# Chunked attention and top-128 mixture-of-depths on one core: the step order written out as a list, V turned back by transposes with separate gate products, 66-column values

## The chip, the cores and the metric

One Trainium2 chip, one of its cores. The metric is device time in microseconds of one execution. The engines are TensorE (PE, with its weight loads shown as PEld), VectorE (DVE), ScalarE (ACT), GpSimd (POOL) and SyncE (SP). Each takes its instructions in the order in which the program issues them, and waits for semaphores of the others. DMAs are issued from POOL (loads, which also turn f32 into f16, gathers and scatters) and from SP (the small loads and the stores).

## The reference

Two stages. First attention in chunks of 32 queries over 768 positions, for 4 batches and 8 heads of 64; each chunk sees 16 positions to its left, itself, 8 to its right, and 8 memory positions.

```python
for c in range(nc):                                   # 24 chunks
    l_start, r_end = max(0, c*32 - 16), min(S, c*32 + 32 + 8)
    k_full = concat([mem_k, k[:, :, l_start:r_end]]); v_full = ...
    a = exp(s - max(s)),  s = q_c @ k_full.T / sqrt(D)
    out[:, :, chunk] = (a / (sum(a) + 1e-9)) @ v_full
```

Its output, with the heads side by side, is x of shape 4 x 768 x 512. Then a routed feed-forward: the 128 positions of each batch with the highest gate score get one.

```python
scores = einsum('bsd,d->bs', x, w_gate)
top = 128 positions with the largest scores[b]
h = maximum(x[b, top] @ w1, 0)                        # 512 -> 1024
out[b, top] = x[b, top] + sigmoid(scores[b, top]) * (h @ w2)
```

## The kernel before

The attention is worked in 16 pairs of heads (NPR = 16, four pairs to a batch). The steps of pair n, by the names of the functions:

- `load` (L92, L96): three DMAs of POOL bring q, k and v into the tiles ldq, ldk and ldv, ten buffers each.
- `t_q`, `c_q`: sixteen PE transposes of q into a bank of PSUM (t, two of them), then two copies, one per head, into the block-diagonal tile qbd (64x384 words of 32 bits), one on ACT and one on DVE (the copying helper is L83 for ACT, L85 for DVE and POOL).
- `t_w`, `c_w`, `m_w` for K and for V: sixteen transposes, one copy into the window tile kw or vw (128x672 words), and a small copy that puts the memory rows in (128x96 words), on POOL.
- `scores` (L258, 26 products), `maxima` (L267, DVE), `sub_max` (L274, two products that add the negative maximum), `expo` (L279, ACT).
- `v_back` (L301): V's windows lie transposed and are turned back by products with a constant tile mvw of 66 columns: the identity and two columns of gate weights. Two halves of twelve products each; `c_vs` copies each half into vs as f16, 128x792 numbers, the first half on ACT, the second on DVE.
- `p_trans`, `c_p`: six transposes of the probabilities, two copies into ptd (64x384 words).
- `values` (L319): 24 products of 67 columns (64 values, two gate columns, a column of ones for the sum); `normal` (L330, L331, L333, DVE) divides into x and into the gate scores gb.

The score tiles, the turned-back V, the probabilities and the values all take one of three double banks w in turn.

Per batch follows the routing: `m_score` sums the gate scores, `m_rows` (L363) transposes them to rows, `m_brow` copies, `m_cmp` (L389, six DVE compares of 768), `m_count` (L397, 36 products of one column), `m_mask`, `m_pref`, `m_select`, `m_aux`, `m_index`, then `m_fetch` gathers the rows (an indirect DMA of POOL), `m_xt` transposes them, `m_ffn1` (L473), `m_relu`, `m_ffn2` (L488), `m_y`, `m_scatter` (L501). For the last batch the rows are picked by products (`m_cast`, `m_pick`, L456) and the scatter adds.

The order is that of one loop, `for i in range(-2, NPR)`: iteration i issues the scores of pair i+1, the values of pair i, the transposes of pair i+2, and a share of the routing of the batch before and of the feed-forward of the one before that (`pieces`). Before the loop the loads of pairs 0 to 8 are issued; after it come batch 2's feed-forward and then all of batch 3's routing. Banks go round by counters (`nw`, `nt`).

Of the kernel before, what the change touches and what calls it, by code (L numbers as in the profile page):

```python
# [25 lines left out]

@with_exitstack
def kernel(  # L30
# [13 lines left out]
    nc = tc.nc  # L44
# [16 lines left out]
    VC = 67  # L61
# [63 lines left out]
    filler(2, 6)  # L125

    ident = cst.tile([128, 128], FP, tag="ident")
    make_identity(nc, ident)
    ident16 = cst.tile([128, 128], F16, tag="ident16")
    DVE.tensor_copy(out=ident16, in_=ident)  # L130
    load("q", 1)
    load("k", 1)
    load("v", 1)
    for t in T:
        DVE.memset(t[:, 0:400], 0.0)
    qbds = [cst.tile([128, NCH, 64], F16, tag=f"qbd{i}", name=f"qbd{i}") for i in range(3)]
    ptds = [cst.tile([128, 6, 4, 2, 32], F16, tag=f"ptd{i}", name=f"ptd{i}") for i in range(3)]
    vss = [cst.tile([128, 12, 2, 68], F16, tag=f"vs{i}", name=f"vs{i}") for i in range(3)]
    for t in qbds:
        DVE.memset(t[0:64, :, 32:64], 0.0)  # L140
        DVE.memset(t[64:128, :, 0:32], 0.0)
    perm16 = cst.tile([128, 128], F16, tag="perm16")
    DVE.tensor_copy(out=perm16.rearrange("p (a t j) -> p a t j", t=4, j=8),
                    in_=ident16.rearrange("p (a j t) -> p a t j", t=4, j=8))
    for t in ptds:
        DVE.memset(t[0:64, :, :, 1, :], 0.0)
        DVE.memset(t[64:128, :, :, 0, :], 0.0)

    slot_i = cst.tile([128, 3], I32, tag="slot_i")
    slot_m = cst.tile([128, 2], FP, tag="slot_m")  # L150
    POOL.iota(slot_i[:, 0:1], pattern=[[0, 1]], base=0, channel_multiplier=1)
    DVE.tensor_scalar(out=slot_i[:, 1:2], in0=slot_i[:, 0:1], scalar1=15, scalar2=None, op0=ALU.bitwise_and)
    DVE.tensor_scalar(out=slot_i[:, 2:3], in0=slot_i[:, 0:1], scalar1=14, scalar2=None, op0=ALU.bitwise_and)
    DVE.tensor_scalar(out=slot_m[:, 0:1], in0=slot_i[:, 1:2], scalar1=3.5, scalar2=None, op0=ALU.is_gt)
    DVE.tensor_scalar(out=slot_m[:, 1:2], in0=slot_i[:, 2:3], scalar1=12.0, scalar2=None, op0=ALU.not_equal)
    for t in vss:
        DVE.memset(t[:, :, :, 66:67], 1.0)
        DVE.tensor_copy(out=t[0:64, 0, :, 66:67], in_=slot_m[0:64, 0:1].unsqueeze(1).to_broadcast([64, 2, 1]))
        DVE.tensor_copy(out=t[64:128, 11, :, 66:67], in_=slot_m[64:128, 1:2].unsqueeze(1).to_broadcast([64, 2, 1]))

    warm = cst.tile([128, 1], FP, tag="warm")
    DVE.memset(warm, 0.0)
    ACT.activation(out=warm, in_=warm, func=AF.Exp, scale=1.0)

    memT = []
    for i in range(2):
        p_m = one(3 + i)[:, 0:128]
        PE.transpose(out=p_m, in_=mem32[i].rearrange("p h d -> p (h d)"), identity=ident)
        mt = cst.tile([128, NPR, 4, 2], F16, tag=f"memT{i}", name=f"memT{i}")
        ACT.copy(out=mt, in_=p_m.rearrange("p (n g j) -> p n j g", n=NPR, j=4))  # L170
        memT.append(mt)

    mvw = cst.tile([128, NP, 66], F16, tag="mvw")
    wgc = cst.tile([128, NP], FP, tag="wgc")

    def gate_weights():
        p_w = one(2)[:, 0:NP]
        PE.transpose(out=p_w, in_=wg4, identity=ident[0:4, 0:4])
        DVE.tensor_copy(out=wgc, in_=p_w)
        for h in range(2):  # L180
            o = 64 * h
            POOL.tensor_copy(out=mvw[o:o + 64, :, 0:64], in_=ident16[o:o + 64, o:o + 64].unsqueeze(1).to_broadcast([64, NP, 64]))
        DVE.tensor_copy(out=mvw[:, :, 64], in_=wgc)
        DVE.tensor_tensor(out=mvw[:, :, 65], in0=wgc, in1=mvw[:, :, 64], op=ALU.subtract)
# [7 lines left out]
    def route_consts():  # L192
# [101 lines left out]
    def v_back(n, half, wi):  # L294
        vw = vws[n]
        w = two(wi)
        for i in range(6):
            P = 6 * half + i
            for h in range(2):
                o = 64 * h  # L300
                PE.matmul(out=w[:, h, 66 * i:66 * i + 66], lhsT=vw[o:o + 64, 2 * P:2 * P + 2].rearrange("p c j s -> p (c j s)"),  # L301
                          rhs=mvw[o:o + 64, n % NP, :], start=True, stop=True)
        pvs[n, half] = w

    def c_vs(n, half, e):
        copy(e, vss[n % 3][:, 6 * half:6 * half + 6, :, 0:66].rearrange("p i h d -> p h i d"),
             pvs[n, half][:, :, 0:396].rearrange("p h (i d) -> p h i d", d=66))
# [364 lines left out]
```

## Time and profile before

| what | value |
|---|---|
| times of three runs | 196.89 us median (195.09 to 199.99) |
| the profiled execution's own time | 197.33 us |
| its span, first to last instruction | 195.6 us |
| mean granted TensorE clock | 0.776 |
| instructions | 5672 |

The span is what all rows of the profile refer to; the rest of the own time lies around it. In the rows of groups, "busy, mean ns | idle before" tells how long an engine worked on a kind of instruction and how long it had stood before it, with the one that ended the wait. Rows of the timeline begin with the start and the length in microseconds.

### The profile page before, as it was taken

The page shows a single profiled execution, that of the slowest core. Times are in us where ns is not written, and L with a number is a line of the kernel's source. Part 1 is how long each engine was busy: PE and PEld are TensorE (multiplying, and loading weights), DVE is VectorE, ACT ScalarE, POOL GpSimd, SP SyncE. Part 2 cuts the span into 40 slices and gives each one's busy share as a digit, 9 for nine tenths or more (in the row PEclk, how much of TensorE's full clock was granted, in tenths as well). Part 3 has the DMA queues.
Part 4 walks back from the last instruction along what each step waited for, and adds up shares of the span by engine and source line. Part 5 has one row for each costly group of instructions (what it writes and reads, how often), then busy time and mean ns, then how long its engine had stood idle before and what let it go on. Part 6 is the DMA issues. An engine that isn't in the chain of part 4 may idle for free. (4 is left out here: it accounts for less than half of the span.)

```text
span 195.6 us, 5672 instructions
## 1 busy us (share of the span) xinstructions
PE 121.0 (62%) x2481; PEld 93.0 (48%) x2481; DVE 121.0 (62%) x259; ACT 60.8 (31%) x101; POOL 60.6 (31%) x113
## 2 busy tenths in 40 slices
PE   5401068567687488889687579895776537516750
PEld 1301046445465467667474458684645436204620
DVE  1872038877855998778429969664599830596010
ACT  2011025365245251541621632534333402100210
POOL 7996697643560000065000501200003020340020
PEclk9999999999658855555869975558899555965797
DMA  3999999999999200029920100730001055000003
GB/s 60 182 197 197 198 198 199 204 201 171 133 298 230 38 3 3 3 42 284 246 38 3 55 3 3 250 129 0 3 0 57 3 179 196 35 18 3 2 0 54
DMA packets 22288, 20.15 MB, mean 103 GB/s; under 512 B 1780, under 2 KB 18168, under 8 KB 22264
## 3 DMA queue, kind: packets, MB, share of 16 engines
q0 software_dynamic: 18416, 13.37, 44.8%
q1 hardware_dynamic: 3848, 6.43, 9.1%
q8 instruction: 19, 0.31, 0.6%
q14 instruction: 5, 0.04, 0.1%
HBM read 23.99 MB, written 7.34 MB: 160 GB/s over the span
## 5 line engine op out<-in xcount | busy, mean ns | idle before, releaser
L501 POOL DMA_INDIRECT out_dram<-y,idx x4 | 5.0, 1261 | 68.6 <-ACT kw L83 40.9
L83 ACT COPY qbd<-t 64x384 uint32<-64x384 uint32 x16 | 7.6, 472 | 47.9 <-PE t L211 47.9
L267 DVE TENSOR_REDUCE nm<-w 128x12 f16<-128x768 f32 x16 | 15.3, 957 | 10.5 <-PE w L258 10.1
L319 PE MATMUL w<-vs,ptd 128*64 128x67 f16 x384 | 12.1, 226 | 15.8 <-DVE ptd L85 15.8
L85 DVE CAST vs<-w 128x792 f16<-128x792 f32 x16 | 15.7, 980 | 8.8 <-PE w L301 8.7
L319 PEld LDWEIGHTS <-ptd 128*64 128x64 f16 x384 | 10.0, 137 | 17.6 <-DVE ptd L85 17.6
L258 PE MATMUL w<-kw,qbd 128*64 128x64 f16 (+2 forms) x416 | 11.7, 214 | 10.2 <-POOL kw L85 10.1
L301 PEld LDWEIGHTS <-vw 64*128 64x128 f16 x384 | 9.4, 108 | 17.6 <-issue 16.8
L301 PE MATMUL w<-mvw,vw 64*128 64x66 f16 x384 | 12.2, 214 | 8.5 <-ACT pp L279 8.5
L473 PE MATMUL w<-xeT,w_sb 128*128 128x128 f16 x128 | 12.4, 275 | 5.5 <-ACT hT L480 2.8
L258 PEld LDWEIGHTS <-qbd 128*64 128x64 f16 x416 | 10.0, 131 | 12.1 <-issue 11.1
L83 ACT CAST vs<-w 128x792 f16<-128x792 f32 x16 | 13.1, 819 | 7.8 <-PE w L301 7.8
L482 DVE TENSOR_SCALAR hT<-w 128x512 f16<-128x512 f32 x4 | 2.8, 692 | 20.6 <-PE w L473 20.6
L437 POOL DMA_INDIRECT xe<-out_dram,idx x3 | 3.1, 1037 | 39.6 <-DVE nm L267 21.0
L333 DVE TENSOR_TENSOR x<-w,rd 128x768 f32<-128x768 f32 x16 | 15.2, 948 | 0.0
L473 PEld LDWEIGHTS <-w_sb 128*128 128x128 f16 x128 | 11.6, 129 | 6.9 <-issue 6.9
L227 PE MATMUL t<-ident,ldv 96*64 96x96 f16 x256 | 10.7, 241 | 5.8 <-DVE qbd L85 5.8
L85 DVE COPY vw<-t 128x672 uint32<-128x672 uint32 x16 | 13.6, 849 | 0.9 <-PE t L227 0.9
L279 ACT ACTIVATE pp<-w 128x768 f16<-128x768 f32 x16 | 13.0, 814 | 3.5 <-PE w L274 3.4
L389 DVE TENSOR_SCALAR gtm<-brow,scr 128x768 f16<-128x768 f32 x24 | 14.0, 633 | 0.1
L85 DVE COPY qbd<-t 64x384 uint32<-64x384 uint32 x16 | 9.0, 561 | 6.1 <-ACT qbd L83 5.8
L211 PE MATMUL t<-ident,ldq 96*64 96x96 f16 x256 | 11.9, 249 | 0.9 <-issue 0.9
(94 smaller groups left out, 245.5 us busy)
## 6 DMA issues: line engine op xcount, KB each, us to landing
out_dram<-x SPq DMA_DIRECT2D x12, 512.0 KB, 5.3
ldq<-in_q_dram POOLq DMA_DIRECT2D x16, 192.0 KB, 6.8
ldk<-in_k_dram POOLq DMA_DIRECT2D x16, 192.0 KB, 7.2
ldv<-in_v_dram POOLq DMA_DIRECT2D x16, 192.0 KB, 7.5
w_sb<-in_moe_w_dram POOLq DMA_DIRECT2D x8, 256.0 KB, 8.2
mem<-in_mem_k_dram SPq DMA_DIRECT2D x2, 32.0 KB, 2.6
mem<-in_mem_v_dram SPq DMA_DIRECT2D x2, 32.0 KB, 4.0
out_dram<-y,idx POOLq DMA_INDIRECT x4, 3.7
```

The source lines that it names most:

```text
L83: ACT.copy(out=out, in_=in_)
L85: ENG[e].tensor_copy(out=out, in_=in_)
L211: PE.transpose(out=tb[64 * h:64 * h + 64, j // 2, j % 2, :], in_=src[:, h, 64 * j:64 * j + 64], identity=ident16[0:96, 0:96])
L227: PE.transpose(out=tb[64 * h:64 * h + 64, j, 4 + 96 * f:100 + 96 * f], in_=src[:, 2 * h + f, 64 * j:64 * j + 64], identity=ident16[0:96, 0 ...
L258: PE.matmul(out=o_, lhsT=qb[:, c, :], rhs=r_, start=(u % 6 == 0 and i == 0), stop=False, skip_group_check=True)
L267: DVE.tensor_reduce(out=nm, in_=sps[n][:, :, 0:384].rearrange("p h (g k) -> p h g k", k=64), axis=AX.X, op=ALU.max, negate=True)
L279: ACT.activation(out=pp.rearrange("p (b u) k -> p b (u k)", b=2), in_=sps.pop(n)[:, :, 0:384], func=AF.Exp, scale=0.125)
L301: PE.matmul(out=w[:, h, 66 * i:66 * i + 66], lhsT=vw[o:o + 64, 2 * P:2 * P + 2].rearrange("p c j s -> p (c j s)"), rhs=mvw[o:o + 64, n % N ...
L319: PE.matmul(out=w[64 * cp:64 * cp + 64, g // 3, u:u + VC], lhsT=pt[:, g, 2 * cp + h].rearrange("p x q -> p (x q)"), rhs=vs[:, 2 * g + cp, ...
L333: DVE.tensor_tensor(out=xs[b][:, :, 128 * pr:128 * pr + 128].rearrange("p (b g) (h d) -> p b g h d", b=2, h=2), in0=p[:, :, :, :, 0:64], i ...
L389: ENG[e].tensor_scalar(out=m.gtm[:, bl, :], in0=m.brow, scalar1=m.scr[:, bl:bl + 1], scalar2=None, op0=ALU.is_lt)
L473: PE.matmul(out=m.p_h[:, half, fi, :], lhsT=w1_sb[:, dch, f0:f0 + 128], rhs=m.xeT[:, dch, :], start=(dch == 0), stop=(dch == 3))
```

## The change

The loop and `pieces` are gone. All work is cut into some 560 steps, and a string `ORDER` names them in the order of issue, with the bank (a digit) or the engine (A for ACT, V for DVE, G for POOL) of each; a function `run` looks each name up. The digits are pairs or batches: `S8:2` is scores of pair 8 in bank 2, `VB` v_back, `VG` the gate products, `CS` the copy into vs, `GS` the sum of gate products, `PT`/`CP` the probabilities, `VA`/`NR` values and normal, `LQ LK LV` loads, `TQ CQ TK CK MK TV CV MV` the transposes, copies and memory rows, `RB BR CM CT MS PP SL PA IX GX XT XE F1 RL F2 YY SX` the routing and feed-forward in the order of the names above, `Z` zero products.

Further, by parts:

- **V back.** `v_back` is 24 f16 transposes into one double bank, 32 words a block; one copy of 128x768 words (`c_vs`) takes the place of the two halves. The gate weights leave that tile: `v_gate` issues twelve products of four columns (two heads, each weight in two f16 parts), `g_sum` adds them on DVE.
- **66 columns.** values has 64 values, one gate column and the ones.
- **Engines.** 17 of the 64x384 copies are on DVE and 47 on ACT (32 and 32 before); 27 of the K and V copies on ACT and 5 on DVE (16 and 16); 19 of the memory-row copies on DVE and 13 on POOL (all 32 on POOL); 15 of the 16 copies into vs on ACT.
- **Zero products.** 18 at the start instead of 6, and six single ones near the end.
- **Small loads.** mem_v is loaded from ACT's queue, mem_k and the gate weights from SP's as before.
- **Feed-forward.** Batch 0's is issued among pairs 12 to 14; batch 1's and 2's after the last values.

```diff
-    for i in range(-2, NPR):
-        a, c, z = pieces(i) if i >= 0 else ([], [], [])
...
+ORDER = """
+Z:2,12 ZT LQ0 LK0 ID I Z:1,6 TQ0:0 ZQ0 CQ0b:A LV0 ZQ1 ZQ2 ZP0 MT0:2 MT1:3 MC1 WR MC0 LK1 LK2 LV1 GT0:4 TK0:1
+CQ0a:V TV0:0 CV0:A CK0:V MV0:V MK0:V GW ZP1 TK1:1 CK1:A S0:3 TK2:0 CK2:A LQ1 LV2 LQ2 VB0:2 MX0 MK2:V ZP2 SI
...
+VB15:3 VG15 PT15:1 PA2:4 CS14:A CS15:A CP15a:A CP15b:A GS14 CP14a:V CP14b:V IX2 GS15 VA14:2 Z:0,1 VA15:4 X60:G
+GX1 XT1:0 XE1:A GX2 Z:1,2 F11:3 NR14 NR15 SC3 RB3:2 BR3:V CM31:V CM33:V CM35:V CM34:V CM32:V CM30:V XT2:1
...
+    def v_back(n, wi):
+        vw = vws[n]
+        w = two(wi)
+        for P in range(12):
             for h in range(2):
                 o = 64 * h
-                PE.matmul(out=w[:, h, 66 * i:66 * i + 66], lhsT=vw[o:o + 64, 2 * P:2 * P + 2].rearrange("p c j s -> p (c j s)"),
-                          rhs=mvw[o:o + 64, n % NP, :], start=True, stop=True)
+                PE.transpose(out=w[:, h, 32 * P:32 * P + 32].bitcast(F16),
+                             in_=vw[o:o + 64, 2 * P:2 * P + 2].rearrange("p c j s -> p (c j s)"),
+                             identity=ident16[o:o + 64, o:o + 64])
+    def v_gate(n):
+        vw = vws.pop(n)
+        for P in range(12):
+            PE.matmul(out=pvs[n][:, 0, 384 + 4 * P:388 + 4 * P],
+                      lhsT=vw[:, 2 * P:2 * P + 2].rearrange("p c j s -> p (c j s)"),
+                      rhs=wgb[:, n % NP, :], start=True, stop=True)
+    def c_vs(n, e):
+        copy(e, vss[n % 3][:, :, :, 0:64].bitcast(U32).rearrange("p i h d -> p h i d"),
+             pvs[n][:, :, 0:384].rearrange("p h (i d) -> p h i d", d=32).bitcast(U32))
+    def g_sum(n):
+        gp = pvs[n][:, 0, 384:432].rearrange("p (i t h) -> p i h t", t=2, h=2)
+            DVE.reduce_sum(out=vss[n % 3][:, :, :, 64:65], in_=gp, axis=AX.X)
```

Where rows stand, engine by engine. First POOL's queue at the start. Before, the last of 27 loads and the first copies of memory rows, which belong to pairs 0 and 1 (kw is K's window tile, memT the transposed memory rows):

```order
L92 DMA ldq_224<-in_q_dram 96x2x512
L96 DMA ldk_226<-in_k_dram 96x4x256
L96 DMA ldv_228<-in_v_dram 96x4x256
L85 COPY kw_264<-memT0_162 128x96
L85 COPY vw_283<-memT1_165 128x96
```

Now, from the sixth load on; the first copy here is that of pair 1, pair 0's having gone to DVE:

```order
L128 DMA ldv_182<-in_v_dram 96x4x256
L124 DMA ldq_294<-in_q_dram 96x2x512
L128 DMA ldv_296<-in_v_dram 96x4x256
L124 DMA ldq_298<-in_q_dram 96x2x512
L653 IOTA slot_i_104 128x1
L117 COPY kw_248<-memT0_107 128x96
L128 DMA ldk_331<-in_k_dram 96x4x256
```

The first copy stands behind nine loads instead of 27, and loads follow it.

Second, DVE in the middle, between two maxima (nm). Before, one pair in early iterations:

```order
L267 TENSOR_REDUCE nm<-w_78 128x12
L330 RECIPROCAL rd<-w_79 128x12
L331 TENSOR_TENSOR gb<-w_79,rd 128x6x4
L333 TENSOR_TENSOR x_460<-w_79,rd 128x6x128
L85 COPY qbd_119<-t_75 64x24x16
L85 CAST vs_127<-w_78 128x2x6x66
L85 COPY vw<-t_75 128x96x7
L85 COPY ptd_124<-w_79 64x24x16
```

Now, from the maxima of pair 7 on:

```order
L302 TENSOR_REDUCE nm<-w_78 128x12
L354 TENSOR_REDUCE vs_103<-w_79 128x24
L377 RECIPROCAL rd<-w_77 128x12
L378 TENSOR_TENSOR gb<-w_77,rd 128x6x2
L380 TENSOR_TENSOR x_1482<-w_77,rd 128x6x128
L377 RECIPROCAL rd<-w_79 128x12
L378 TENSOR_TENSOR gb<-w_79,rd 128x6x2
L380 TENSOR_TENSOR x_1482<-w_79,rd 128x6x128
L117 COPY kw<-memT_107 128x96
L354 TENSOR_REDUCE vs_101<-w_77 128x24
```

The copy into vs and that of vw are gone from here; the sum of gate products (into vs, 128x24) and a copy of memory rows have come, and two pairs' normal stand together.

Third, DVE at the end, where the last batch's scores (scr) are summed. Before:

```order
L357 TENSOR_REDUCE scr<-gb 128x6
L482 TENSOR_SCALAR hT<-w_78 128x512
L494 SCALAR_TENSOR_TENSOR y<-w_79,gate,xe 128x512
L378 TENSOR_SCALAR gt<-gt 128x6
L379 RECIPROCAL gt<-gt 128x6
L381 CAST aux_174<-gt 128x6
L382 TENSOR_TENSOR aux_174<-gt,aux_174 128x6
L389 TENSOR_SCALAR gtm<-brow,scr 128x768 x6
```

Now:

```order
L449 TENSOR_REDUCE scr<-gb 128x6
L117 COPY brow<-w_77 128x768
L481 TENSOR_SCALAR gtm<-brow,scr 128x768 x6
L575 TENSOR_SCALAR hT<-w_79 128x512
L587 SCALAR_TENSOR_TENSOR y<-t_75,gate,xe 128x512
L495 TENSOR_SCALAR mask<-w_77 128x6
```

Batch 2's relu (hT) and its y no longer stand ahead of the compares (gtm), and the four instructions of the gate (gt, aux) have moved behind the selection; the row copy (brow) has come over from ACT.

On PE the same place reads: the row transposes (L455) come after the first half of batch 1's first product (L566), and between them and the counts (L489) stand batch 2's transposes, the other half, both halves of batch 2's first product, and batch 1's second product (L581).

More of the change, by code (lines that the diff above doesn't have):

```diff
@@ L29 @@
+"""
 @with_exitstack
@@ L122 @@
     wg4 = cst.tile([4, 128], FP, tag="wg4")
     SP.dma_start(out=wg4, in_=_dap(moe_w_gate, 0, [[128, 4], [1, 128]]))
-    filler(2, 6)
     ident = cst.tile([128, 128], FP, tag="ident")
-    make_identity(nc, ident)
     ident16 = cst.tile([128, 128], F16, tag="ident16")
[L130 to L135, printed above, removed]
+    perm16 = cst.tile([128, 128], F16, tag="perm16")
     qbds = [cst.tile([128, NCH, 64], F16, tag=f"qbd{i}", name=f"qbd{i}") for i in range(3)]
@@ L154 @@
[L154 to L159, printed above, removed]
@@ L161 @@
-    warm = cst.tile([128, 1], FP, tag="warm")
[L162 to L173, printed above, removed]
@@ L174, with z_t @@
-    wgc = cst.tile([128, NP], FP, tag="wgc")
[L176 to L179, printed above, removed]
+    warm = cst.tile([128, 1], FP, tag="warm")
+    memT = [cst.tile([128, NPR, 4, 2], F16, tag=f"memT{i}", name=f"memT{i}") for i in range(2)]
+    wgb = cst.tile([128, NP, 4], F16, tag="wgb")
+    wgc = cst.tile([128, NP], FP, tag="wgc")
+    p_ms = {}
+    def z_t():
+        for t in T:
+            DVE.memset(t[:, 0:400], 0.0)
@@ new lines, in act_warm, with mem_t, mem_c, g_trans @@
+    def act_warm():
+        ACT.activation(out=warm, in_=zero[:, 0:1], func=AF.Exp, scale=1.0)
+    def mem_t(i, bk):
+        p_ms[i] = one(bk)[:, 0:128]
+        PE.transpose(out=p_ms[i], in_=mem32[i].rearrange("p h d -> p (h d)"), identity=ident)
+    def mem_c(i):
+        ACT.copy(out=memT[i], in_=p_ms[i].rearrange("p (n g j) -> p n j g", n=NPR, j=4))
+    def g_trans(bk):
+        p_ms["w"] = one(bk)[:, 0:NP]
+        PE.transpose(out=p_ms["w"], in_=wg4, identity=ident[0:4, 0:4])
+    def g_weights():
+        DVE.memset(wgb, 0.0)
+        DVE.tensor_copy(out=wgc, in_=p_ms["w"])
@@ new lines, in values_only @@
+    def values_only(n, wi):
+        pt, vs = ptds[n % 3], vss[n % 3]
+        w = two(wi)
+        pxs[n] = w
+        for g in range(6):
+            for h in range(2):
+                for cp in range(2):
+                    u = 64 * (2 * (g % 3) + h)
+                    PE.matmul(out=w[64 * cp:64 * cp + 64, g // 3, u:u + 64],
+                              lhsT=pt[:, g, 2 * cp + h].rearrange("p x q -> p (x q)"),
+                              rhs=vs[:, 2 * g + cp, h, 0:64], start=True, stop=True)
@@ L336, with normal_only @@
+    def normal_only(n):
+        b, pr = divmod(n, NP)
+        if b not in xs:
+            xs[b] = xpool.tile([128, 6, Dm], FP, tag="x", name=f"x{b}")
+        p = pxs.pop(n)[:, :, 0:384].rearrange("p b (g h d) -> p b g h d", h=2, d=64)
+        DVE.tensor_tensor(out=xs[b][:, :, 128 * pr:128 * pr + 128].rearrange("p (b g) (h d) -> p b g h d", b=2, h=2),
+                          in0=p, in1=rds[n].unsqueeze(4).to_broadcast([128, 2, 3, 2, 64]), op=ALU.mult)
     class MS:
@@ new lines @@
+    NONE = {"ZT": z_t, "ID": lambda: make_identity(nc, ident), "I": i_16, "PM": p_16, "VI": vs_init, "WR": act_warm,
+            "GW": g_weights, "RC": r_pool, "RD": r_dve,
+            "SI": lambda: POOL.iota(slot_i[:, 0:1], pattern=[[0, 1]], base=0, channel_multiplier=1)}
+    for item in ORDER.split():
+        name, _, arg = item.partition(":")
+        if name == "Z":
+            bk, cnt = arg.split(",")
+            filler(int(bk), int(cnt))
+        else:
+            run(name, arg if arg in ("A", "V", "G") else None, int(arg) if arg.isdigit() else None)
```

302 lines of the change are left out of this document (138 added, 164 removed).

## Prediction

> **What bounds the kernel now.** I read the page's head first, then the table of windows for three stretches.
>
> ```profile
> span 195.6 us, 5672 instructions
> PE 121.0 (62%) x2481; PEld 93.0 (48%) x2481; DVE 121.0 (62%) x259; ACT 60.8 (31%) x101; POOL 60.6 (31%) x113
> PEclk9999999999658855555869975558899555965797
> ```
> TensorE (PE) and VectorE (DVE) are busy equally long, each 62% of the span; so neither is the bound of the whole, and the order in which the queues wait for one another must be. The clock row shows that TensorE ran at half clock about half of the time from the middle on.
>
> The same by stretch; columns are the stretch and its length, busy time of PE, PEld, DVE, ACT and POOL with instructions in brackets, granted clock, DMA share, GB/s.
>
> ```profile
> 0.00:27.10 27.10, 7.01 (x90) 4.26 (x92) 9.73 (x39) 2.78 (x6) 21.88 (x48) 1.00 1.18 170
> 27.10:157.30 130.20, 97.01 (x2241) 76.24 (x2236) 98.56 (x193) 54.04 (x88) 32.54 (x61) 0.75 0.51 101
> 157.30:195.60 38.30, 16.97 (x157) 12.49 (x157) 12.73 (x28) 3.96 (x7) 6.22 (x7) 0.72 0.21 62
> ```
> The cuts are the first maxima (the DVE's reduction over scores of pair 0, at 27.1) and the end of the last pair's values product (157.3). **Start:** 27.1 us in which PE works 7 and DVE 10. **Middle:** sixteen pairs in 130.2 us, PE busy 75%, DVE 76%, at clock 0.75. **End:** 38.3 us in which no engine is busy even half of the time: one chain. Each of the three gives a term.
>
> **Start: 27.1 becomes 13.5.** From the timeline: start, length, engine, instruction, and in brackets idle time before it and who ended that.
>
> ```profile
> 1.26 2.74 PE L113 MATMUL w<-zero 128*128 128x512 f16 x6 [1.26 <-DVE zero L109]
> 8.55 0.84 PE L227 MATMUL t<-ident,ldk 96*64 96x96 f16 x16
> 24.14 0.68 POOL L96 DMA_DIRECT2D ldk<-in_k_dram  x1 [0.34 <-DMA ldv<-in_v_dram]
> 25.77 0.37 POOL L85 COPY kw<-memT 128x96 uint32<-128x96 uint32 x1
> 26.19 0.87 PE L258 MATMUL w<-kw,qbd 128*64 128x48 f16 x26 [10.10 <-POOL kw L85]
> 27.09 0.96 DVE L267 TENSOR_REDUCE nm<-w 128x12 f16<-128x768 f32 x1 [10.11 <-PE w L258]
> ldk<-in_k_dram POOLq DMA_DIRECT2D x16, 192.0 KB, 7.2
> ```
> The keys of pair 0 were transposed at 8.55, but scores waited until 26.19 for a 0.37 us copy of memory rows on GpSimd (POOL), which stood in its queue behind the loads of pairs 3 to 8, and those were paced by the DMA. The change issues that copy for pair 0 on the DVE, and for pair 1 on POOL behind nine loads, not 27. What is left in front, at half clock: 18 zero products instead of 6 (0.42 each, to 9.0), q's transposes, three single ones at a zero product's 0.4 and k's (0.84 + 1.2 + 0.84, to 11.9), the copy of kw on DVE (0.85, row below) and two copies of memory rows (0.5, bounded by POOL's 0.37 each), scores 0.87: first maxima at about 14.1. If the clock opens under the zero products after some 4 us, the last eight take half, they end by 7.3 and all of it comes by 12.5. The loads (7.2 us from issue to landing) are there: K0's transposes ran at 8.55 already. I take **13.5**, a gain of 13.6. Nothing hides this: DVE and PE had stood 10.1 us.
>
> **Middle: 130.2 becomes 105.** First the engines' work, by groups (busy us, mean ns of one | idle before).
>
> ```profile
> L85 DVE CAST vs<-w 128x792 f16<-128x792 f32 x16 | 15.7, 980 | 8.8 <-PE w L301 8.7
> L83 ACT CAST vs<-w 128x792 f16<-128x792 f32 x16 | 13.1, 819 | 7.8 <-PE w L301 7.8
> L301 PE MATMUL w<-mvw,vw 64*128 64x66 f16 x384 | 12.2, 214 | 8.5 <-ACT pp L279 8.5
> L227 PE MATMUL t<-ident,ldv 96*64 96x96 f16 x256 | 10.7, 241 | 5.8 <-DVE qbd L85 5.8
> L85 DVE COPY vw<-t 128x672 uint32<-128x672 uint32 x16 | 13.6, 849 | 0.9 <-PE t L227 0.9
> L83 ACT COPY kw<-t 128x672 uint32<-128x672 uint32 x16 | 11.5, 719 | 1.9 <-PE t L227 0.9 <-DVE x L333 0.7
> L85 DVE COPY qbd<-t 64x384 uint32<-64x384 uint32 x16 | 9.0, 561 | 6.1 <-ACT qbd L83 5.8
> L83 ACT COPY qbd<-t 64x384 uint32<-64x384 uint32 x16 | 7.6, 472 | 47.9 <-PE t L211 47.9
> L357 DVE TENSOR_REDUCE scr<-gb 128x6 f32<-128x96 f32 x4 | 1.0, 251 | 0.1
> ```
> DVE: the sixteen vs casts go (-15.7) and one whole copy is left (+1.0); sixteen sums of gate products come, 24 results from 48 numbers, priced by the 0.251 of the nearest small reduction (+4.0; by none at all 0, by the largest reduction here, the maxima's 0.96, 15). Of 32 copies of form 64x384 (qbd, ptd), 17 stay on DVE (15 x 0.561 = -8.4); of sixteen vw copies five V or K copies stay (11 x 0.849 = -9.3); 19 memory-row copies come over from POOL, at 0.25 each, between zero and POOL's 0.37 (+4.8). 98.6 - 15.7 + 1.0 + 4.0 - 8.4 - 9.3 + 4.8 = **75**. Start-up memsets that slide into the stretch and batch 1's relu and y that leave it nearly cancel.
>
> ACT: fifteen copies of all of vs (768 numbers, 32-bit words that hold two f16, so all twelve row blocks in the time of six) instead of sixteen halves, and the 15 and 11 copies: 54.0 - 13.1 + 15 x 0.819 + 15 x 0.472 + 11 x 0.719 = **68**.
>
> PE: 384 products become 384 transposes of the same number (mean 214 against 241 ns with their latency, overlapped: between no change and 384 x 27 ns = 10 us, taken at 0 since in a row they overlap, sixteen in 0.53 us, below), and 192 gate products come, of four columns. The nearest are the count's one-column products, 31 in 0.98 us (row further down), so +6.1; above, at 214 ns each unoverlapped, 41. Batch 1's feed-forward leaves the stretch (two of 1.05 and one of 2.06, rows below: -4.2). 97.0 + 6.1 - 4.2 = **99** at that stretch's clock. What the clock is worth:
>
> ```profile
> 47.76 0.53 PE L227 MATMUL t<-ident,ldv 96*64 96x96 f16 x16
> 29.30:49.80 20.50, 13.68 (x460) 10.58 (x454) 16.88 (x27) 10.90 (x18) 12.17 (x24) 1.00 1.27 189
> 66.90:94.20 27.30, 23.32 (x487) 18.94 (x489) 21.88 (x45) 10.31 (x17) 5.54 (x10) 0.50 0.30 74
> 43.20:46.60 3.40, 2.18 (x70) 1.56 (x71) 3.27 (x7) 1.03 (x2) 1.91 (x4) 1.00 1.21 177
> 46.60:50.00 3.40, 1.79 (x60) 1.46 (x59) 2.27 (x4) 2.00 (x4) 1.93 (x4) 1.00 1.02 144
> 84.10:87.50 3.40, 3.10 (x68) 2.24 (x65) 2.54 (x5) 1.80 (x3) 2.50 (x4) 0.50 0.27 28
> 90.95:94.35 3.40, 3.40 (x58) 3.00 (x60) 2.37 (x5) 0.95 (x2) 0.00 (x0) 0.50 1.16 285
> ```
> Sixteen transposes took 0.53 here and 0.84 in the start, 1.6 times. With half of the middle at either clock, 99 is 76 at full and 122 at half clock. So at full clock three engines have 75, 76 and 68 us to do in the same stretch, and at half clock PE alone has 122. How near to that can an order come? At full clock the old one kept DVE busy 16.88 of 20.5 (82%); 75 / 0.82 = 92, and with three engines level I take 95. At half clock it kept PE busy 23.32 of 27.3 (85%); the new order has other products between each copy and the product that needs it, so I take 90%: 135.
>
> Which clock? The windows of 3.4 us tell: after one with PE busy 2.18 it stayed full, after 1.79 it fell; at half clock 3.10 did not open it, 3.40 did. At full clock the new order asks 76 of 95, or 2.7 of 3.4, above both; where it falls, a PE that no longer waits comes near 3.4. I give a quarter of the work to half clock: 0.75 x 95 + 0.25 x 135 = **105**. The Trainium skill (TensorE: Matmul & The Clock Gate, Part 1) has the gate open after one busy window of about 3.4 us and close after an idle one; the rows agree on the length, and add that 53% busy is idle enough. Part 4 of that page speaks against this change: transposes do not count as busy in the same way, and V's way back turns from products into transposes. By that rule the first rival below decides, and the sum is its 181; the half-clock window with 3.10 of 3.40 busy that opened nothing speaks for it, the window held at full clock by 2.18 against.
>
> **End: 38.3 becomes 28.**
>
> ```profile
> 158.53 0.24 DVE L357 TENSOR_REDUCE scr<-gb 128x6 f32<-128x96 f32 x1
> 160.15 1.11 PE L444 MATMUL w<-ident,xe 128*128 128x128 f32 x4 [2.89 <-DMA xe<-out_dram,idx]
> 168.00 0.82 PE L363 MATMUL w<-ident,scr 128*128 128x128 f32 x6
> 169.79 3.58 DVE L378 TENSOR_SCALAR gt<-gt 128x6 f32<-128x6 f32 x1 [0.84 <-ACT gt L374]
> 170.20 3.14 POOL L85 CAST x<-x 128x768 f16<-128x768 f32 x4
> 173.92 3.26 DVE L389 TENSOR_SCALAR gtm<-brow,scr 128x768 f16<-128x768 f32 x6
> 177.24 0.98 PE L397 MATMUL w<-ones,gtm 128*128 128x1 f16 x31 [0.34 <-DVE gtm L389]
> 180.33 2.72 PE L456 MATMUL w<-sel,x 128*128 128x128 f16 x24
> 183.76 1.05 PE L473 MATMUL w<-xeT,w_sb 128*128 128x128 f16 x16 [0.72 <-ACT xeT L83]
> 186.44 2.06 PE L488 MATMUL w<-w_sb,hT 128*128 128x512 f16 x8
> 189.50 1.63 POOL L501 DMA_INDIRECT out_dram<-y,idx  x1 [16.17 <-ACT y L496]
> ```
> Batch 3's scores were summed at 158.5, but the transposes of its rows stood behind batch 2's gather and feed-forward until 168.0: 9.2 us. From 168.0 to the end, 27.6, is the true chain, and in it one DVE instruction of six numbers took 3.58 beside POOL's casts, so that the compares began at 173.9 instead of about 169.8. In the new order batch 3's row transposes wait only for batch 1's four transposes, a copy of 512 numbers (0.7, under the 0.82 of 792) and half of its first product: 1.1 + 0.7 + 1.05, or 2.8 after the last values product. Then 27.6, less 4.1 (gate moved behind the selection), less 1.0 (24 picks at full clock after the feed-forward, 1.7 for 2.72), plus 2.1 (batch 1's second product stands in front of the counts on PE, which now end later than the compares), plus 0.8 (batch 2's second product, 2.06, goes between counts and picks, which the old chain has 2.1 apart, 178.2 to 180.3, but it begins only behind the prefix product in there): 25.4. Together **28**; 26 if the added products are covered, 31 at half clock, where eight products of 512 columns take 3.4 by the zero products' 0.42, 1.3 more, twice or thrice. The casts on POOL come before the compares begin; if all four met them they would cost their 3.14 again. The Trainium skill (Advanced Engine Details and Errata, VectorE Performance Modes) has the second Vector port shared with GpSimd, which the 3.58 beside 3.14 bears out; it would move the end to 31.
>
> **Sum.** 13.5 + 105 + 28 = 146.5 of span; the profiled execution's own time was 197.33 for 195.6, 1.7 more: **148**. It stands 0.2% above the median of the runs shown, 196.89, so nothing is corrected. About 2% is what measurement of this kernel can tell from no change.
>
> **Rivals.**
> - PE at half clock throughout: 13.5 + 135 + 31 + 1.7 = 181. For it: half of the old middle, and batch 1's feed-forward, dense PE work, has left that stretch. Against: a denser PE. Chance 0.15, with 165 to 181 for mixtures.
> - The order leaves hardly a bubble: the middle at 82, the start at 12.5, the end at 27: 123. For it: in the middle no engine has over 76. Against: the old 82%. 0.12.
> - The new order is a list made for durations of a model, and in-order queues stall where they differ: the middle stays 130 and only start and end gain: 173. 0.07.
> - **Slower:** POOL's queue again. Thirteen memory-row copies are still in it, most of them between loads; if at each the loads behind come late by most of the 7.2 us to landing, say 5, then 13 x 5 = 65 is added: 213. It decides from the point where a copy's wait is longer than the lead of the loads in flight; for it speaks the old start, against it that in the new list a pair's loads stand pairs ahead of their use, and that POOL was busy 32.5 of 130.2 in the middle. 0.04.
>
> Forecast 0.62, from 132 to 165. The range: 132 to 173 leaves out the bubble-free case's lower part (0.07) and most of the half-clock and slower cases (0.13). Faster by over 2% (below 193): all but the last and some unforeseen, 0.94; within 2% 0.02; slower 0.04.
>
> **What would show it.** First maxima at 12.5 to 14.5, no PE wait for POOL of several us in the start; DVE's vs casts gone, its busy time in the middle near 75, ACT near 68; gate products about 0.35 a dozen; mean clock above 0.8 in the middle; last values product near 119, batch 3's row transposes within 3 us of it. Wrong would be: first maxima after 18, clock below 0.65 in the middle, PE waiting on DMA landings there, or a new wait of PE for ACT as long as those removed.

## The result, and the profile after

The changed kernel takes 141.75 us (median of four runs, 139.7 to 142.8), the kernel before 197.02 beside it: a ratio of 0.716, 95% interval 0.701 to 0.731. 148 was predicted, with a range from 132 to 173. The profiled execution's own time is 141.96, its span 140.0. Some executions of a kernel are 1.5 to 4% slower than its others: the ratios given here leave these out, the medians do not, and the profiled one of the changed kernel is among them.

The head of the page, with the clock row and the row of the instruction queue (packets, MB, share of 16 engines):

```profile
span 140.0 us, 6033 instructions
PE 110.2 (79%) x2691; PEld 86.3 (62%) x2691; DVE 90.8 (65%) x254; ACT 75.0 (54%) x128; POOL 53.6 (38%) x91
PEclk9999999959559999556998555579999999999996
q8 instruction: 21, 0.34, 0.9%
```

PE is now ahead of DVE, 79% against 65% of the span, and half clock is left in four patches. The table of windows, cut as before at the first maxima and at the end of the last pair's values product:

```profile
0.00:11.21 11.21, 8.88 (x131) 4.82 (x133) 7.36 (x25) 3.72 (x7) 9.57 (x21) 1.00 0.92 126
11.21:114.16 102.95, 84.61 (x2361) 69.44 (x2360) 71.38 (x197) 65.77 (x111) 38.84 (x66) 0.82 0.86 156
114.16:140.00 25.84, 16.72 (x207) 12.06 (x206) 12.10 (x33) 5.55 (x10) 5.20 (x5) 0.95 0.33 103
```

| stretch | before | predicted | after |
|---|---|---|---|
| start | 27.1 | 13.5 | 11.2 |
| middle | 130.2 | 105 | 103.0 |
| end | 38.3 | 28 | 25.8 |

In the timeline of PE, in the start and in the middle (start, length, instruction; in brackets the idle time before it):

```profile
1.27 4.16 PE L145 MATMUL w<-zero 128*128 128x512 f16 x12 [1.27 <-DVE zero L141]
5.26 1.46 PE L145 MATMUL t<-zero 128*128 128x512 f16 x6
6.65 0.53 PE L246 MATMUL t<-ident,ldq 96*64 96x96 f16 x16
9.73 0.57 PE L293 MATMUL w<-kw,qbd 128*64 128x48 f16 x26
...
21.33 0.33 PE L335 MATMUL w<-ident,vw 64*128 64x64 f16 x11 [1.55 <-issue]
27.53 0.33 PE L246 MATMUL t<-ident,ldq 96*64 96x96 f16 x7 [1.05 <-issue]
33.73 0.80 PE L335 MATMUL w<-ident,vw 64*128 64x64 f16 x43 [1.51 <-issue]
56.83 0.23 PE L335 MATMUL w<-ident,vw 64*128 64x64 f16 x1 [2.85 <-issue]
74.04 0.42 PE L293 MATMUL w<-kw,qbd 128*64 128x64 f16 x14 [2.40 <-issue]
```

The last five rows are a kind of wait that hardly occurred before (three of 0.23 to 0.43 us there, at products 350, 478 and 606). PE stands still inside a group of equal products, for which all data is there, and the profile names no releaser. I counted the products of the trace: the stalls lie ahead of numbers 350, 478, 606, 1118, 1502 and, with 0.44 us, 1630. These differ by multiples of 128. A product with its weight load is two instructions, and the page's 21 instruction packets for 2 x 2691 of them make 256 each, 16 KB. So each of these stalls is at the border of two instruction packets. In the trace's DMA records the packet of product 1118 starts at 54.47, half a microsecond after PE had stopped at 53.98, and that of 1502 at 71.64, the very moment PE stopped. In each of the six, PE goes on 1.2 to 1.5 us after the record of its packet has ended, and in none of the fourteen traces here does product 94 + 128 k start less than 1.1 us after the record of the k-th packet has ended. With the short sixth one the stalls cost 9.8 us, and each of the four clock falls follows a window of 3.4 us that has one in it (PE busy 0.52, 0.46, 0.45 and 0.52 of it). The second and the third of these windows:

```profile
31.43:34.85 3.42, 1.58 (x78) 1.37 (x73) 2.17 (x4) 1.96 (x4) 2.90 (x5) 1.00 0.91 115
51.92:55.33 3.41, 1.52 (x51) 1.05 (x48) 2.71 (x8) 2.06 (x4) 0.64 (x1) 1.00 1.35 229
```

### The profile page after: what moved, and what is told of

Its sections match the earlier page's. It is cut to its first block, busy times and chain, and to the rows that moved or that the text cites. A ratio compares the mean times of both kernels' runs of the same rounds, so it can differ in the third digit from the quotient of the medians.

```text
span 140.0 us, 6033 instructions
## 1 busy us (share of the span) xinstructions
PE 110.2 (79%) x2691; PEld 86.3 (62%) x2691; DVE 90.8 (65%) x254; ACT 75.0 (54%) x128; POOL 53.6 (38%) x91
## 3 DMA queue, kind: packets, MB, share of 16 engines
q1 hardware_dynamic: 3560, 6.36, 12.5%
## 5 line engine op out<-in xcount | busy, mean ns | idle before, releaser
L115 ACT COPY vs<-w 128x768 uint32<-128x768 uint32 x15 | 12.2, 810 | 10.4 <-PE w L343 6.9
L335 PE MATMUL w<-ident,vw 64*128 64x64 f16 x384 | 10.0, 202 | 6.6 <-issue 5.9
L380 DVE TENSOR_TENSOR x<-w,rd 128x768 f32<-128x768 f32 x16 | 15.1, 947 | 0.0
L115 ACT COPY ptd<-w 64x384 uint32<-64x384 uint32 x23 | 10.9, 474 | 6.0 <-PE w L321 4.7
L354 DVE TENSOR_REDUCE vs<-w 128x24 f16<-128x48 f32 x16 | 4.2, 265 | 14.3 <-ACT vs L115 11.2
L366 PE MATMUL w<-vs,ptd 128*64 128x66 f16 x384 | 11.0, 214 | 2.2 <-DVE vs L354 1.4
L124 POOL DMA_DIRECT2D ldq<-in_q_dram x16 | 10.5, 659 | 4.2 <-DMA w_sb<-in_moe_w_dram 2.2
L128 POOL DMA_DIRECT2D ldv<-in_v_dram x16 | 11.3, 705 | 2.0 <-DMA ldk<-in_k_dram 0.8
L115 ACT COPY vw<-t 128x672 uint32<-128x672 uint32 x14 | 10.1, 722 | 3.6 <-PE t L262 2.9
L128 POOL DMA_DIRECT2D ldk<-in_k_dram x16 | 10.9, 683 | 1.9 <-DMA ldq<-in_q_dram 0.9
L115 ACT COPY kw<-t 128x672 uint32<-128x672 uint32 x13 | 9.3, 718 | 3.9 <-PE t L262 3.4
L262 PE MATMUL t<-ident,ldk 96*64 96x96 f16 x256 | 10.8, 240 | 0.8 <-DVE wgc L213 0.5
```

What stands on the lines that cost most here:

```text
L115: ACT.copy(out=out, in_=in_)
L124: POOL.dma_start(out=t, in_=_dap(q, 2 * n * HD, [[512, 96], [HD, 2], [1, 512]]))
L128: POOL.dma_start(out=t, in_=_dap(src, 2 * n * HD, [[256, 96], [HD // 2, 4], [1, 256]]))
L262: PE.transpose(out=tb[64 * h:64 * h + 64, j, 4 + 96 * f:100 + 96 * f], in_=src[:, 2 * h + f, 64 * j:64 * j + 64], identity=ident16[0:96, 0 ...
L335: PE.transpose(out=w[:, h, 32 * P:32 * P + 32].bitcast(F16), in_=vw[o:o + 64, 2 * P:2 * P + 2].rearrange("p c j s -> p (c j s)"), identity ...
L366: PE.matmul(out=w[64 * cp:64 * cp + 64, g // 3, u:u + VC], lhsT=pt[:, g, 2 * cp + h].rearrange("p x q -> p (x q)"), rhs=vs[:, 2 * g + cp, ...
```

## The experiments

**The two ends, within the old loop.** The memory rows of pairs 0 and 1 on DVE; behind the loop batch 3's rows and compares first.

```diff
-            m_w("k", i + 2, "G")
+            m_w("k", i + 2, "V" if i < 0 else "G")
...
-    m_xt(b, nw())                      # batch 2's feed-forward, then batch 3's routing
+    m_rows(b, nw()); m_brow(b, "A")    # batch 3
+    for pr in range(NP): m_cast(b, pr, "G")
+    m_gexp(b); m_cmp(b, 0, 6)
+    m_xt(b2, nw())                     # batch 2's feed-forward; counts and picks within it, gate after the picks
```

> The kernel before, its loop and its V back unchanged, with only its two ends mended: the memory rows of pairs 0 and 1 are copied by DVE instead of POOL, and behind the loop batch 3's row transposes and compares are issued ahead of batch 2's feed-forward, with the gate behind the picks. Theory (three separate gains: start, middle, end): first maxima at about 17 instead of 27.1, the end stretch about 30 instead of 38.3, the middle still 130: about 178 us. Rival (the gain belongs to the list as a whole, the ends are held by something else, such as DMA landings in the start): 190 or more.

Measured: 178.6 us. Its windows:

```profile
0.00:17.03 17.03, 7.09 (x96) 4.44 (x98) 10.02 (x41) 2.79 (x6) 14.91 (x33) 1.00 1.06 153
17.03:147.04 130.01, 95.57 (x2236) 74.28 (x2231) 99.64 (x196) 53.64 (x88) 37.77 (x71) 0.77 0.61 117
147.04:176.97 29.93, 16.83 (x157) 12.04 (x157) 8.54 (x27) 4.50 (x8) 6.27 (x7) 0.67 0.27 80
```

The start falls by 10.1 us, the end by 8.4, the middle stays at 130.0: as expected. Both causes that the prediction named for the ends are shown, each by a few moved lines; the list takes another 5.8 us from the start and 4.1 from the end.

**V back, within the old loop**, on top of that: transposes, gate products, one copy on ACT and the sum on DVE in place of the two halves.

```diff
-            v_back(i + 1, 0, w)
-            c_vs(i + 1, 0, "A")
-            w = nw()
-            v_back(i + 1, 1, w)
-            c_vs(i + 1, 1, "V")
+            v_back(i + 1, nw())
+            v_gate(i + 1)
+            c_vs(i + 1, "A")
+            g_sum(i + 1)
```

> As loop_ends, and in the same loop V back by 24 transposes, gate products, one copy on ACT and a sum on DVE, as in the changed kernel. Theory (rebalancing gives part of the middle, the order the rest): DVE's 15.7 us of copies into vs go and some 4 come; the loop's waits keep part of that, the middle comes to about 121: 169 us. Rival A (the order alone makes the middle shorter): the middle stays 130, 178 us. Rival B (V back is the whole gain of the middle): the middle comes near 105, 153 us.

Measured: 179.2 us. The middle, and PE's longest waits in it with the two ends alone (first fence: waits in all, times, longest), then with V back as well (second):

```profile
PE w L319 <- DVE ptd L85: 15.1, 15, 2.2
PE w L301 <- ACT pp L279: 9.0, 10, 1.2
```

```profile
17.36:146.29 128.93, 100.71 (x2428) 80.89 (x2423) 87.51 (x196) 53.58 (x88) 37.83 (x71) 0.79 0.61 117
PE w L331 <- DVE ptd L85: 9.5, 14, 1.4
PE w L300 <- ACT pp L279: 3.8, 3, 1.3
PE w L258 <- issue: 3.1, 2, 2.1
PE t L227 <- issue: 1.6, 1, 1.6
```

DVE loses 12 us of work and the middle gets 1.1 us shorter. Rival A holds: within the loop V back is worth next to nothing. Its products wait less for copies, but PE has 5 us more to do (100.7 for 95.6), and stalls at instruction packets appear (products 478, 606 and 734, 4.8 us; with the two ends alone the borders cost 0.6).

**The new order with the old V back**: halves of twelve products in one bank, one after the other.

```diff
-        elif f in ("CS", "BR"):
-            {"CS": c_vs, "BR": m_brow}[f](n, e)
+        elif f == "VB":
+            vbk[n] = bk
+            v_back(n, 0, bk)
+            c_vs(n, 0, "A")
+        elif f == "CS":
+            v_back(n, 1, vbk[n])
+            c_vs(n, 1, "V")
```

> The changed kernel's order with the old V back: two halves of twelve products of 66 columns in one double bank after the other, two copies of 128x792 numbers (ACT, then DVE), no gate products and no gate sums, 67 columns of values. Theory: DVE gets 15.7 back and loses 4.2, and TensorE waits for the first copy before the second half; the middle comes to 115 to 120 instead of 103: 155 to 160 us. Rival A (the order alone): 143. Rival B (V back is everything): 170.

Measured: 151.1 us (149.0 and 153.2), span 147.1.

```profile
11.47:120.64 109.17, 80.71 (x2155) 64.28 (x2156) 82.98 (x199) 65.98 (x112) 38.19 (x65) 0.84 0.80 147
```

It was a miss on the low side, between the theory and rival A. The middle is 109.2, so of its 27 us the order (with its division of the copies among the engines) brings 21 without the new V back, and the new V back the last 6. The two are not a sum: V back is worth 1 us in the loop and 6 in this order. That this is because only here PE no longer stands waiting for other copies is argued, not shown: in both places the new V back also brings stalls, which with the old one are nearly absent (0.5 us at the borders in this run, 9.8 in the changed kernel).

**Without most loads.** The stalls suggest that PE's instructions come late because their packets wait among data.

```diff
     def load(nm, n):
+        if n >= 3:
+            lds[nm, n] = kept[nm, n % 3]
+            return
```

> The changed kernel without the loads of pairs 3 to 15: these pairs work on q, k and v of pairs 0 to 2, so that part of the input is left out; every instruction of the engines stays but POOL's 39 load issues. In the changed kernel TensorE stands still in the middle of groups of products, at product 350, 478, 606, 1118, 1502 and 1630, all a multiple of 128 apart, 9.8 us in all, each time just as a 16 KB instruction packet comes late among data packets; and the four windows after which the clock fell to half each hold one of these stalls. Theory (the instruction packets wait behind data): without most of the data the stalls go, the clock stays full, the middle comes from 103 to about 87: 125 us. Rival (the stalls have another cause, or the clock falls for lack of work): stalls stay at the same products, 138 to 142 us.

Measured: 136.0 us (134.4 and 137.6), the middle 97.8.

```profile
54.01 0.23 PE L338 MATMUL w<-ident,vw 64*128 64x64 f16 x1 [2.16 <-issue]
76.72 0.46 PE L296 MATMUL w<-kw,qbd 128*64 128x64 f16 x17 [2.49 <-issue]
PE w L346 <- DVE vs L117: 2.3, 1, 2.3
```

Between theory and rival. Four stalls are gone (350, 478, 606, 1502); product 1118 keeps one, at 51.9, and that of 1630 grows from 0.4 to 2.5 us, at 74.2, both just where stores of 1.5 MB and two or three loads of weights, which this kernel still has, were on their way. So data in front of the packet is shown as the cause. That the clock would stay full was wrong: two falls follow these two stalls, another the 2.3 us wait for DVE in the third row, and a fourth a window without a long wait (80.51 to 83.92, PE busy 0.79 of it).

**Fewer instructions** (`merged_v` in the expectations that follow). V back by twelve transposes over all 128 rows.

```diff
-            for h in range(2):
-                o = 64 * h
-                PE.transpose(out=w[:, h, 32 * P:32 * P + 32].bitcast(F16), in_=vw[o:o + 64, 2 * P:2 * P + 2]...,
-                             identity=ident16[o:o + 64, o:o + 64])
+            PE.transpose(out=w[:, P // 6, 64 * (P % 6):64 * (P % 6) + 64].bitcast(F16), in_=vw[:, 2 * P:2 * P + 2]...,
+                         identity=ident16)
```

> The changed kernel with V turned back by twelve transposes of both heads at once (128 rows by 128 columns) instead of 24 of one head: 192 fewer products and as many fewer weight loads of 2691 each, so one instruction packet of 14 less. Theory (TensorE's instructions are brought in packets that come late): the stalls move to other products and lose about a tenth, TensorE's work stays as it is (six 128x128 transposes of probabilities take 0.51 us, 24 small ones 0.52): 138 to 141 us. Rival (two small ones of different rows run side by side, so twelve whole ones take twice as long): +0.5 us a pair, 150 us.

Measured: 136.9 us, less than both had expected, ratio 0.688 (0.675 to 0.700) to the kernel before, wholly below that of the changed kernel. The transposes as a group in the changed kernel, and here:

```profile
L335 PE MATMUL w<-ident,vw 64*128 64x64 f16 x384 | 10.0, 202 | 6.6 <-issue 5.9 <-ACT ptd L115 0.4
```

```profile
L333 PE MATMUL w<-ident,vw 128*128 128x128 f16 x192 | 14.3, 230 | 1.0 <-ACT ptd L115 0.4 <-DVE vs L351 0.4
28.15 0.54 PE L363 MATMUL w<-vs,ptd 128*64 128x66 f16 x23 [1.42 <-issue]
40.54 0.82 PE L363 MATMUL w<-vs,ptd 128*64 128x66 f16 x23 [2.03 <-issue]
64.07 0.92 PE L486 MATMUL w<-ones,gtm 128*128 128x1 f16 x29 [1.19 <-issue]
```

The group costs PE 4.3 us more, 0.27 a pair where the rival had 0.5, and the kernel is faster all the same: the stalls fall from 9.8 to 5.6 us, by far more than the theory's tenth, and half clock in the middle from 37.5 to 13.7. The stalls lie at products 350, 478, 734, 1246 and 1374, the same borders of 128, though other instructions stand there now. That settles what they are; how much of the gain is due to fewer instructions, and how much to where the packets happened to meet data, it leaves open.

**Pacing the loads, and holding back stores.** Three load buffers for ten, and the memory rows on DVE (`MK..:G` to `:V`); then that with the twelve transposes and stores held back.

```diff
-    ld = ctx.enter_context(tc.tile_pool(name="ld", bufs=10))
+    ld = ctx.enter_context(tc.tile_pool(name="ld", bufs=3))
...
+    def tie(n):                        # in SP's queue ahead of the second and third store of a batch
+        SP.dma_start(out=tied[:, n:n + 1], in_=nms[n][0:1, 0, 0:1])
```

> The changed kernel with three load buffers for each of q, k and v instead of ten, so that a pair's loads start when the pair three before it has been transposed, and with the 13 memory-row copies that were still on POOL moved to DVE, so that POOL's queue holds no loads back and sends them in no bursts. All data is loaded. Theory (instruction packets wait behind a pile of data packets): the stalls at products 350, 478, 606 and 1502 go, those beside the stores of batches 0 and 1 stay, DVE has 3.4 us more: 135 to 138 us. Rival (loads come too late with three buffers, or DVE's work decides): TensorE waits for landings, 145 us or more.

> As paced, with the twelve whole transposes of merged_v, and the second and third store of batches 0 and 1 held back by a two-byte DMA in SP's queue that reads the maxima of a later pair (7 and 8, 11 and 12). Theory: no pile of data packets is left in the middle, no stall over 1 us without a releaser, the clock falls at most once: 130 to 134 us. Rival (the stalls only move, engine waits take their place): 137 or more.

Measured: 149.2 and 141.0 us; both missed, and the first is slower than the changed kernel. PE's longest waits in the first:

```profile
PE w L293 <- issue: 3.2, 2, 2.8
PE t L246 <- DMA ldq<-in_q_dram: 2.8, 2, 2.4
```

Landings now hold PE (2.8 us before transposes of q), and DVE's copies into kw and vw (1.2 to 1.6). The stalls at products 350, 478 and 606 went, as the theory had it, but that at 1502 stayed (2.8 us) and one of 1.4 came late in the middle, and a load of k still takes 6.1 us from issue to landing for 7.4. In time the rival was right, in both runs.

**Without the zero products at the start** (`Z:2,12` and `Z:1,6` struck out), in the changed kernel and in the one with twelve transposes:

> The changed kernel without the 18 zero products at the start (the six near the end stay). Theory (the zero products open the clock): the first transposes run at half clock, sixteen in 0.84 instead of 0.53 us, first maxima at 12 to 13 instead of 11.2, and half clock lasts into the first pairs: 143 to 146 us. Rival (the start waits for DMA landings and DVE): first maxima at 11.2, 141 to 142 us.

> merged_v without the 18 zero products at the start. Theory (the zero products buy nothing: without them the changed kernel had its first maxima 0.5 us later and took 139.4 for 141.8; the difference in the middle came from where the stalls for instruction packets fell): 135 to 138 us, the same as merged_v's 136.9 within 1%. Rival (18 products fewer ahead of the instruction packets, or a shifted clock window, are a gain of their own): 134 or less.

Measured: 139.4 us, less than both had expected; and 138.3, ratio 0.703 (0.696 to 0.710), beside 136.9 with them, about as the theory had it. First maxima at 11.72 for 11.21, and 11.70. The zero products buy half a microsecond at the start and no time that can be measured. The first rows without them:

```profile
5.51 0.85 PE L246 MATMUL t<-ident,ldq 96*64 96x96 f16 x16 [5.51 <-DMA ldq<-in_q_dram]
9.71 0.91 PE L293 MATMUL w<-kw,qbd 128*64 128x48 f16 x26
```

PE waits for q until 5.5 in any case; then it takes 0.85 for 0.53 a group, and is little later at the scores, since it waits for other engines and for landings in between in both kernels.

The two runs also bear on the twelve transposes: without the zero products these are worth 1.1 us between the medians (138.3 for 139.4, from runs of 138.2 and 140.7), with them 4.8. That fewer instructions gain time by themselves is therefore not shown.

**The gate sum ahead of the copy.** The largest wait of a computing engine in the changed kernel's middle is DVE's before the sum, 11.2 us. The sum does not use the copy's result, but both read one bank of w, and the program lets one engine after the other into it.

```profile
DVE vs L354 <- ACT vs L115: 11.2, 6, 3.6
```

```diff
-CS2:V VG2 CV4:A MV4:V GS2
+VG2 GS2 CS2:V CV4:A MV4:V
```

> merged_v with the gate sum on DVE issued ahead of the copy into vs in ten of the sixteen pairs, where it stood behind it; both read one bank of PSUM and go one after the other, and the sum takes 0.27 us, the copy 0.81. DVE stood 8.3 us before these sums for ACT's copies. Theory (DVE's wait is beside the path, which TensorE and its instruction packets set): 136 to 138 us, DVE's wait gone and a wait of ACT in its place. Rival (the wait is on the path): 130 to 133 us.

(The sum or the copy was moved in twelve pairs; the expectation miscounts.) Measured: 141.1 us, ratio 0.718 (0.709 to 0.727), slower than merged_v. Both expected times were wrong; that a wait of ACT would take the place of DVE's came true. DVE's 8.3 us before the sums become 6.0, now for PE, and ACT waits 10.7 us in DVE's stead:

```profile
ACT vs L115 <- DVE vs L351: 10.7, 11, 2.5
DVE vs L351 <- PE w L340: 6.0, 4, 2.8
```

The long wait was not what set the time. That ACT's new wait is the cause of the 4 us lost is argued only.

**Only the stores held back**, with the twelve transposes and all ten buffers; then pair 7's memory rows behind the four loads that waited for them on POOL (`MV7:G` moved behind `LK11`).

> merged_v with the second and third store of batches 0 and 1 held back in SP's queue, by a two-byte DMA that reads the maxima of pairs 7 and 8, 11 and 12. Theory (the instruction packet waits behind all data issued before it): the stores no longer meet the loads that POOL issues at 44 to 56 and 59 to 72 us, the stall at product 1246 goes: 134 to 136 us. Rival (the loads alone fill the engines, as with three buffers): 136 to 138 us.

> merged_tied with one step moved: the copy of pair 7's memory rows into vw, for which POOL's queue stood 6.8 us while the DMA engines were idle, is issued behind the four loads that stood behind it (q of pair 11, a quarter of w2, v of pair 10, k of pair 11), so that these go out at about 35 instead of 42.7 us and no longer pile up with the loads after them. Theory (instruction packets wait behind piled data): the backlog between 43 and 60 us is four loads shorter, the stall at product 1246 goes: 131 to 133 us. Rival (the loads only fill the idle time, the stalls fall elsewhere): 134 us, no change.

Measured: 134.1 us, ratio 0.682 (0.676 to 0.689), and 133.4, ratio 0.671 (0.662 to 0.679). Both beat the changed kernel; the second is the fastest version here, though by the intervals it is apart neither from the first nor from merged_v (0.675 to 0.700). That holding the stores back is worth the 2.8 us between the medians is therefore likely, not shown. Its middle and its stalls:

```profile
11.39:105.48 94.09, 79.78 (x2163) 66.57 (x2160) 72.43 (x200) 64.94 (x111) 38.29 (x66) 0.95 0.93 170
21.52 0.37 PE L246 MATMUL t<-ident,ldq 96*64 96x96 f16 x9 [0.37 <-issue]
40.66 0.54 PE L363 MATMUL w<-vs,ptd 128*64 128x66 f16 x23 [1.03 <-issue]
68.21 0.36 PE L246 MATMUL t<-ident,ldq 96*64 96x96 f16 x8 [1.75 <-issue]
```

The middle is 8.9 us shorter than in the changed kernel, the stalls 3.3 us in all for 9.8, the clock 0.95 for 0.82. In detail the first expectation failed: with the stores held back the stall at product 1246 stayed (1.5 us) and others shrank; it went with the moved loads, and one at 1374 came.

## Why the prediction was right

**The three terms.** Each came within 2.3 us, and each erred towards too long. That the start and the end were waits of their own, with the causes named, is shown by the two ends mended within the loop (-10.1 and -8.4 us, the middle unmoved).

**Start, 11.2 for 13.5.** The clock opened under the zero products, as the prediction's second case had it: the first sixteen transposes take 0.53 us. Its time for that case, 12.5, was still 1.3 too long, and that by its own sum: it takes the gain off the zero products alone (7.3 for 9.0) and leaves all behind them at half clock. With q's and k's transposes at 0.53, three single products at 0.2 and the scores at 0.57, the same sum gives 10.9. No wait of PE for POOL was left. The zero products end at 6.7, 1.2 us after q lands (5.5 without them), so they do stand in front of the chain, but what follows at full clock makes up for that and for half a microsecond more.

**Middle, 103.0 for 105.** The work came out as summed or below: DVE 71.4 for 75, ACT 65.8 for 68, PE 84.6 at clock 0.82 between the 76 and 122 of the two clocks. The predicted mean clock was above 0.8, the time at half clock 0.25 x 135 = 34 us, measured 37.5. That the sum came so near is in part luck, since its three factors were off in ways that cancel: a third of the products was worked at half clock (788 there, 1598 at full clock), not a quarter; at the rate measured there the whole middle would have taken 114 us, not 135, and at the rate of full clock 98, not 95. The rows of DVE that were priced by others:

```profile
L354 DVE TENSOR_REDUCE vs<-w 128x24 f16<-128x48 f32 x16 | 4.2, 265 | 14.3 <-ACT vs L115 11.2 <-PE w L343 3.0
L117 DVE COPY vw<-memT 128x96 uint32<-128x96 uint32 x10 | 2.6, 264 | 0.0
```

The sums of gate products took 4.2 us (+4.0 predicted), a memory-row copy on DVE 0.264 (0.25), a dozen gate products 0.45 (0.35). What the term had wrong is its reason for the falls of the clock and for part of the idle time. The prediction looked for too little work per window; the windows did fall at 45% to 52% busy, but each has a stall at an instruction packet in it, which the prediction did not know, and without which PE would have been busy 0.83 of it or more (an estimate, the stall added to the busy time). Of the 15.1 us that PE stood at full clock, 7.9 are such stalls; the allowance of 82% had been read off the old order, where PE waited for copies. A middle without any bubble was its rival at 82; the best version here comes to 94.1.

**The rule that spoke against the change.** Between 62.15 and 65.57, at half clock, PE was busy throughout, two thirds of it with transposes, and full clock followed; but after three equally full windows later it did not (75.81 to 79.22, and two more):

```profile
62.15:65.57 3.42, 3.42 (x78) 2.99 (x77) 3.00 (x7) 1.81 (x3) 3.30 (x6) 0.50 0.89 113
82.63:86.05 3.42, 3.42 (x66) 2.39 (x64) 1.31 (x2) 1.44 (x3) 0.00 (x0) 0.50 0.03 7
86.05:89.46 3.41, 3.41 (x94) 3.01 (x92) 3.11 (x10) 3.17 (x8) 0.87 (x1) 0.50 0.00 0
```

So half clock throughout, 181 us, did not come. By the Trainium skill (TensorE: Matmul & The Clock Gate, Part 4: transposes don't count as busy in the same way) the first window should not have opened the clock; by its Part 1 (one busy window opens it) the other two should have. Neither holds alone here. That transposes count is shown by a window of the kernel with only the stores held back, in which PE does nothing else (16 of k, twelve of V back, 16 of v, 16 of q); full clock followed it:

```profile
11.12:14.53 3.41, 3.41 (x60) 3.08 (x60) 2.45 (x6) 0.72 (x1) 2.40 (x5) 0.50 1.32 193
```

What fits the traces is the work that the array gets in a window. For each product that starts in it, take the columns that it streams, times its share of the array's 128 rows and 128 columns; a transpose that the profile writes as 96*64 96x96 counts 96 x 96/128 x 64/128 = 36. In the changed kernel the windows at half clock with 3160 to 3456 were followed by full clock, those with 2970 and less were not (the two above have 2952 and 2970, the one of transposes alone 3192); at full clock it fell after 2688, 2208 and 2296 and stayed after 2912 and more. Over all fourteen traces one bound, 2900, sorts 426 of the 444 windows that hold no f32 products; PE's busy time, with a bound of its own for each clock, sorts 398. This is a fit to these traces, and no run was made to test it.

**End, 25.8 for 28.** In the timelines of PE and DVE:

```profile
113.59 0.57 PE L366 MATMUL w<-vs,ptd 128*64 128x66 f16 x24 [0.24 <-ACT ptd L115]
116.90 0.87 PE L455 MATMUL w<-ident,scr 128*128 128x128 f32 x6 [0.43 <-DVE scr L449]
118.80 3.27 DVE L481 TENSOR_SCALAR gtm<-brow,scr 128x768 f16<-128x768 f32 x6
120.72 1.89 PE L581 MATMUL t<-w_sb,hT 128*128 128x512 f16 x8
122.45 1.04 PE L489 MATMUL w<-ones,gtm 128*128 128x1 f16 x36
```

The row transposes begin 2.7 us after the last values product (2.8 predicted). Batch 1's part on PE is over after 2.3; the last 0.43 is a wait that the term did not have, for DVE, which divides two pairs and sums the scores. From there to the end it is 23.1 us for 25.4. The mis-sized step is batch 1's second product, +2.1: it runs at 120.72, under the compares, which end at 122.07, and delays the counts by 0.4 at most. The prediction's own 26 for covered products was right. POOL's casts were over before the compares.

**The slower rival**, POOL's queue, did not happen: POOL stood up to 9 us before a memory-row copy, but the loads behind it had pairs of lead. In the last experiment four of these loads were let past: 133.4 for 134.1, not apart.

## What to carry to other kernels

Cut the span at its stages first: a chain at either end is mended by a few moved lines, and what a change pays that takes work off an engine depends on the order around it (V back: 1 us in the loop, 6 in the list, beside the stalls that it brings). Look for idle time inside a group of equal products with no releaser, count the products between such places, and when they are a fixed number apart, look for the data that the instructions wait behind: without most loads the stalls halved (9.8 to 4.7 us). Fewer instructions and stores kept away from bursts of loads gave the fastest version here, though neither is shown to gain by itself. Don't go by the length of a wait alone: moving DVE's longest (8.3 us in merged_v) made the kernel slower.

## What was not expected of the hardware

- TensorE's instructions come in packets of 256 over the DMA engines. While loads filled these, packets came some 6.0 us apart (13.13, 19.14, 25.07 and 31.34 in the changed kernel's DMA records), which is 128 products in 6 us; a pair of the changed kernel has about 150 (2361 in its middle).
- The row of granted clock reads 1.00 from the start, even without zero products, where sixteen transposes take 0.85 us and not 0.53. At the start the duration of a known instruction tells the clock, not the row.
- Twelve transposes of 128 rows cost PE 14.3 us over all pairs, 24 of 64 rows 10.0: the small ones of the two heads overlap, as the Trainium skill has it of products in different rows of the array (TensorE: Matmul & The Clock Gate, Part 3). The kernel with the twelve was 4.8 us faster all the same with the zero products at the start, and 1.1 without them.
